# Block-sparse attention and a top-1 MoE on one core: wider exponential tiles, filler matmuls in four early steps, and one of the x copies moved to VectorE

## The chip, the cores and the metric

The kernel runs on one core of one Trainium2 chip. The metric is the device time of one execution in microseconds (us), as the median of several runs. Times inside an execution are in us from the start of its span, and durations of single instructions are in ns where that is said.

## The reference, cut to what matters

The inputs are q, k, v of shape (4, 8, 768, 64), that is 4 batches, 8 heads, 768 positions and a head size of 64, and the weights of an MoE with 8 experts. Everything is fp32.

```python
k_sum = k.reshape(B, H, nb, 32, D).max(axis=3)
v_sum = v.reshape(B, H, nb, 32, D).mean(axis=3)
scores_l = where(|i - j| < 16, scale * q @ k.T, -1e9)
scores_s = scale * q @ k_sum.T + log(32)
a = softmax(concat([scores_l, scores_s]))
x = a @ concat([v, v_sum])
e[s] = argmax(x @ w_gate) where the local gate is below 0.5, else e[s-1]
out[s] = p[e] * relu(x[s] @ w1[e]) @ w2[e]
```

Each position attends to the 31 positions around it and to 24 block summaries. Its row of x (512 wide, all heads) then goes through one expert, 512 to 1024 to 512.

## The kernel before

**Attention** is done for 16 pairs of heads (4 batches by 4 pairs), and for each pair in two groups of three query tiles of 128 positions, so there are 32 groups, G = 0 to 31. A query tile is taken as two halves of 64 positions; each half sees a window of 96 keys and the 24 summaries, W = 120 columns. TensorE (PE) does three things for a group:

- `s_mm` (lines 286 and 292): adds a mask by a matmul with an identity and then multiplies q by the window, into a score tile in PSUM. There are two score tiles, used in turn.
- `t_stage` (through the helper `halves`, line 536): transposes the exponentials. They lie in `pr`, a tile of 128 positions by 2 heads by 3 tiles by WE = W + 1 = 121 columns; the last column is a constant one, which multiplies the 1e-9 of the softmax's denominator. Every transpose takes the exponentials of 64 positions as the stationary operand (64 rows, 121 columns) and a 64x64 identity as the moving one. Rows 0 to 63 and rows 64 to 127 of the array work side by side, each into its own PSUM bank, so 12 transposes are 6 pairs. For one group of each pair of heads two more transposes follow, of `va`, the sums of v, which have the same width. ScalarE (ACT) copies the two banks to `pt`, one after the other (line 538).
- `a_mm` (line 326): multiplies `pt` by the window of v, `vw`.

The groups are software-pipelined by hand: in step G of the loop PE is given `s_mm(G)`, `t_stage(G-2)` and `a_mm(G-3)` in this order. VectorE (DVE) finds the row maximum (`s_max`, line 298), ACT takes six exponentials of 128x120 (`s_exp`, line 306), and DVE divides by the denominator (`a_norm`, lines 337 and 338). GpSimd (POOL) prepares what later pairs need, in this order for each pair of heads: four copies of the v summaries into `vw` (line 264, they need `pt`), three copies of key windows into `kb` (line 255), two additions that fold v (line 241), and the key summaries into `kb` (line 258, they need a reduction on DVE, line 231). SP issues the loads of q, k, v and `vw`; how far they run ahead is set by the buffers (two of `kb`, `kp` and `vt`, three of q and `vw`). Every engine takes its instructions in order.

**Between attention steps** the work of the previous batch's MoE is inserted. After every batch but the last, in three steps that follow one another (G = 10, 11, 12 after the first batch, and 8 and 16 later), `x_two` takes two tiles of x (128 positions by 512) and transposes them for the gate, also through `halves`: 16 transposes of 64 rows by 128 columns into the same two PSUM banks, copied by ACT to `hs` as two copies of 128x512, c = 0 and c = 1. `x_logits` (lines 565 to 576) multiplies `hs` by the gate's weights in these steps and the next two. The routing itself is a long chain of small DVE instructions with a few PE steps.

**The MoE** starts with the last attention steps and takes the time from 125 us to the end: pairs of blocks of 128 tokens, whose matmuls split fp32 into a high and a low part (lines 1176 to 1178 and 1206 to 1208).

At the start of the program 44 matmuls of a zero tile `wz` (128x128, bf16, line 214) run before the first data arrive.

Of the kernel before, what the change touches and what calls it, by code (L numbers as in the profile page):

```python
# [19 lines left out]
P = 128  # L20
# [2 lines left out]
NB = S // 32  # L23
WL = 96
W = WL + NB
WE = W + 1
NU = S // P
NG = 3
GP = NU // NG
# [14 lines left out]
DRAINS = 5  # L44
OOB = 4096
WARM = 44

WFETCH = (21, 21, 22, 22, 26, 30)
WSPLIT = (25, 29)
# [25 lines left out]
class Kernel:  # L75
# [91 lines left out]
    def attention(self, tick, rows, tail):  # L167
        nc, tc, ident = self.nc, self.tc, self.ident
        with ExitStack() as ctx:
# [13 lines left out]
            vts, kss, vss = {}, {}, {}  # L183
            vas = [cst.tile([P, WE], F32, name=f"va{i}") for i in range(3)]

            def load_k(n):
                b, p = pairs[n]
                nc.sync.dma_start(out=kp[n % 2][:, 16:16 + S], in_=self.kT[b, p])
# [14 lines left out]
            for t in vas:  # L203
                nc.gpsimd.memset(t, 0.0)
            prs = [cst.tile([P, 2, NG, WE], F32, name=f"pr{i}") for i in range(2)]
            for t in prs:
                nc.gpsimd.memset(t[:, :, :, W:WE], 1.0)
            for t in kp:
                nc.vector.memset(t[:, 0:16], 0.0)
                nc.vector.memset(t[:, 16 + S:], 0.0)  # L210

            wb = self.bank("t")
            for _ in range(WARM):
                nc.tensor.matmul(out=wb[:, 0:P], lhsT=self.wz, rhs=self.wz, start=True, stop=True)
            load_k(0)
            nc.scalar.dma_start(out=me, in_=self.maskc)

# [3 lines left out]
            t, src = next(consts)  # L221
# [49 lines left out]
            def s_mm(G):  # L271

                n, g = groups[G]
                sp = live[G] = self.score[G % 2].tile([P, 2, 512], F32, name="bs")
                quarters = [(h, c) for c in range(2) for h in range(2)]

                def at(h, c):
                    u = sp[64 * c:64 * c + 64, h, 0:NG * W].rearrange("p (u w) -> p u w", u=NG)  # L280
                    return slice(64 * h, 64 * h + 64), u

                for h, c in quarters:
                    r, o = at(h, c)
                    m0 = W * (2 * g + c)
                    nc.tensor.matmul(out=o.rearrange("p u w -> p (u w)"), lhsT=eye2[r], rhs=mask2[r, m0:m0 + NG * W],
                                     start=True, stop=False)
                for u in range(NG):
                    for h, c in quarters:
                        r, o = at(h, c)  # L290
                        t = 2 * (NG * g + u) + c
                        nc.tensor.matmul(out=o[:, u, :], lhsT=qs[n % 3][r, 64 * t:64 * t + 64], rhs=kb[n % 2][r, t, :],
                                         start=False, stop=(u == NG - 1))
# [16 lines left out]
            def t_stage(G, n=None):  # L310
                pr = live[G]
                pt = live[G] = wk.tile([WE, 2 * NG + 1, P], F32, name="pt", bufs=3)
                srcs = [pr[:, h, u, :] for h in range(2) for u in range(NG)]
                if n is not None:
                    srcs.append(vas[n % 3])
                    vss[n] = pt[0:NB, 2 * NG, :]
                self.halves(srcs, WE, pt[:, 0:len(srcs)])

            def a_mm(G):
# [3 lines left out]
                for u in range(NG):  # L323
                    for h in range(2):
                        for c in range(2):
                            nc.tensor.matmul(out=ap[64 * c:64 * c + 64, u, h, :], lhsT=pt[:, NG * h + u, 64 * c:64 * c + 64],
                                             rhs=vw[n % 3][0:WE, 2 * (NG * g + u) + c, h, :], start=True, stop=True)

# [25 lines left out]
            for G in range(last_g):  # L354
                if G == last_g - GP - 1:
                    ctx3.close()
                s_mm(G)
                tick(G, 2)
                tick(G, 4)
# [5 lines left out]
                if LT <= G:  # L365
                    n = G // 2 - 1 if G in (2, 4) else G // GP if G > 2 * GP and G % GP == 0 or G == 2 * GP + 1 else None
# [12 lines left out]
                n, g = divmod(G, GP)  # L379
# [145 lines left out]
            self.nc.tensor.transpose(out=m[:, P * c:P * c + P], in_=x[:, u % NG, P * c:P * c + P], identity=self.ident)  # L525
        return m

    def halves(self, srcs, m, dst):

        half = P // 2  # L530
        n = len(srcs)
        banks = [self.bank("t")[:m, 0:half * n].rearrange("p (i q) -> p i q", q=half) for c in range(2)]
        for i, src in enumerate(srcs):
            for c in range(2):
                r = slice(half * c, half * c + half)
                self.nc.tensor.transpose(out=banks[c][:, i], in_=src[r], identity=self.ident[r, r])  # L536
        for c in range(2):
            self.nc.scalar.copy(out=dst[:, :, half * c:half * c + half], in_=banks[c])  # L538

    def hs_of(self, b, u):  # L540
        if (b, u // 2) not in self.hs:
# [8 lines left out]
    def x_two(self, b, u):  # L550

        self.hs_of(b, u)
        srcs = [self.xs[b, v // NG][:, v % NG, P * c:P * c + P] for v in (u, u + 1) for c in range(KT)]
        self.halves(srcs, P, self.hs[b, u // 2].rearrange("p j k t -> p (j k) t"))

    def x_logits(self, b, g):

# [1074 lines left out]
```

## Time and profile before

| | |
|---|---|
| runs | 444.4, 445.69 and 446.58 us, median 445.69 |
| the profiled execution | 447.26 us |
| its span, first to last instruction | 445.5 us |
| mean granted clock of TensorE | 0.981 of 2.4 GHz |
| PE busy | 423.7 us (95%) |
| weight loads (PEld) busy | 371.2 us (83%) |
| DVE, ACT, POOL busy | 242.1, 201.0 and 214.8 us |
| moved by DMA | 95.87 MB, mean 215 GB/s |

The profile is of one execution, and its span leaves out 1.8 us that lie around it. A busy PE is not a PE at its peak: matmuls overlap in the array, and several small ones side by side count as one busy time. The clock has two levels, 2.4 GHz (a granted clock of 1.00) and 1.2 GHz (0.50); a value between the two means that part of the stretch ran at the lower one.

### The profile page before, as it was taken

How to read it: one execution, taken by the hardware profiler on the slowest of the kernel's cores; microseconds unless marked ns; L12 is line 12 of the kernel's file. 1: busy time of each engine (PE TensorE's matmuls, PEld its weight loads, DVE VectorE, ACT ScalarE, POOL GpSimd, SP SyncE). 2: the span in 40 equal slices, each digit the busy share in tenths (PEclk: the TensorE clock that was granted, in tenths of full speed). 3: DMA queues.
4: the chain of work that ended last, by engine and by line, in shares of the span. 5: the costliest groups of instructions: out<-in, count | busy, mean ns of one | idle time of the engine just before them, and what ended most of it. 6: DMA issues, size and time to landing. Idle time of an engine off the chain costs nothing. (4 is left out here: it accounts for less than half of the span.)

```text
span 445.5 us, 12679 instructions
## 1 busy us (share of the span) xinstructions
PE 423.7 (95%) x4750; PEld 371.2 (83%) x4750; DVE 242.1 (54%) x577; ACT 201.0 (45%) x441; POOL 214.8 (48%) x310
## 2 busy tenths in 40 slices
PE   7989999988999999999999999999999999999992
PEld 6867788777889889898989889889897898978982
DVE  4657578797668578976531221223736652164720
ACT  3848678686865322712121201114536731276610
POOL 3387567568721430872012210211939792077960
PEclk9669999999999999999999999999999999999998
DMA  8899989999516192156056047200573876029581
GB/s 299 338 366 321 391 288 313 359 385 407 169 49 237 49 381 93 61 214 270 25 214 267 31 141 310 72 29 16 206 253 118 358 276 246 24 59 380 213 325 57
DMA packets 24007, 95.87 MB, mean 215 GB/s; under 512 B 2894, under 2 KB 3536, under 8 KB 19312
## 3 DMA queue, kind: packets, MB, share of 16 engines
q1 hardware_dynamic: 19328, 80.30, 48.4%
q0 software_dynamic: 4448, 14.29, 9.3%
q8 instruction: 44, 0.72, 0.7%
q14 instruction: 43, 0.35, 0.2%
q10 hardware_dynamic: 144, 0.20, 0.1%
HBM read 82.20 MB, written 12.71 MB: 213 GB/s over the span
## 5 line engine op out<-in xcount | busy, mean ns | idle before, releaser
L1206 PE MATMUL bs<-xT,h 128*128 128x256 f32 x352 | 101.6, 289 | 0.0
L1207 PE MATMUL bs<-xT,h 128*128 128x256 f32 x352 | 99.7, 283 | 0.0
L1208 PE MATMUL bs<-xT,l 128*128 128x256 f32 x352 | 99.6, 283 | 0.0
L1145 POOL DMA_INDIRECT xg<-x_dram,gidx x30 | 33.5, 1117 | 85.6 <-PE bt L1156 30.2
L1139 POOL TENSOR_TENSOR l<-stg,h 128x256 fp32r<-128x256 f32 x72 | 66.8, 963 | 15.3 <-ACT h L1131 14.7
L1176 PE MATMUL ba<-h,hT 128*128 128x512 f32 x176 | 71.5, 406 | 0.4
L1212 ACT ACTIVATE hT<-bs 128x512 fp32r<-128x512 f32 x44 | 26.3, 597 | 96.5 <-PE bs L1208 93.3
L1178 PE MATMUL ba<-h,hT 128*128 128x512 f32 x176 | 68.9, 392 | 0.0
L1177 PE MATMUL ba<-l,hT 128*128 128x512 f32 x176 | 68.8, 391 | 0.0
L1206 PEld LDWEIGHTS bs<-xT,h 128*128 128x128 f32 x352 | 67.5, 192 | 1.5 <-issue 0.8
L1207 PEld LDWEIGHTS bs<-xT,h 128*128 128x128 f32 x352 | 67.5, 192 | 0.3
L1214 DVE SCALAR_TENSOR_TENSOR hT<-bs,hT 128x512 fp32r<-128x512 f32 x44 | 30.4, 691 | 68.3 <-ACT hT L1212 56.0
L1208 PEld LDWEIGHTS bs<-xT,l 128*128 128x128 f32 x352 | 67.5, 192 | 0.0
L306 ACT ACTIVATE pr<-bs,nm 128x120 f32<-128x120 f32 x192 | 52.3, 389 | 6.0 <-DVE nm L298 3.9
L1131 ACT CAST h<-stg 128x1024 fp32r<-128x1024 f32 x48 | 49.0, 1051 | 9.3 <-PE ba L1178 7.6
L1192 POOL DMA_INDIRECT out_dram<-yo,sidx x24 | 25.0, 1043 | 49.6 <-DMA out_dram<-yo,sidx 12.0
L1134 DVE TENSOR_TENSOR l<-stg,h 128x1024 fp32r<-128x1024 f32 x30 | 40.2, 1351 | 12.6 <-ACT h L1131 9.4
L538 ACT COPY pt<-bt 121x448 f32<-121x448 f32 (+1 forms) x64 | 29.4, 515 | 25.4 <-PE bt L536 23.4
L1176 PEld LDWEIGHTS ba<-h,hT 128*128 128x128 f32 x176 | 33.2, 188 | 7.4 <-issue 0.6
L1178 PEld LDWEIGHTS ba<-h,hT 128*128 128x128 f32 x176 | 33.1, 188 | 7.2
L1177 PEld LDWEIGHTS ba<-l,hT 128*128 128x128 f32 x176 | 33.2, 189 | 5.6
L264 POOL COPY vw<-pt 24x384 f32<-24x384 f32 x64 | 30.3, 514 | 8.9 <-ACT pt L538 8.0
(307 smaller groups left out, 673.8 us busy)
## 6 DMA issues: line engine op xcount, KB each, us to landing
stg<-in_w SPq DMA_DIRECT2D x28, 1024.0 KB, 7.3
vw<-in_vW SPq DMA_DIRECT2D x16, 780.0 KB, 6.7
few_w<-in_w SPq DMA_DIRECT2D x8, 1024.0 KB, 8.1
kp<-in_kT SPq DMA_DIRECT2D x16, 384.0 KB, 6.7
q<-in_qT SPq DMA_DIRECT2D x16, 384.0 KB, 7.3
vt<-in_vT SPq DMA_DIRECT2D x16, 384.0 KB, 7.2
x_dram<-xs SPq DMA_DIRECT2D x8, 768.0 KB, 5.4
wst<-in_w SPq DMA_DIRECT2D x8, 512.0 KB, 6.6
```

Of the source, the lines that this page charges most:

```text
L306: nc.scalar.activation(out=pr[:, h, u, 0:W], in_=sp[:, h, u, :], func=AF.Exp, bias=nm[:, h, u:u + 1], scale=1.0)
L1131: self.nc.scalar.copy(out=hi, in_=src)
L1134: eng.tensor_tensor(out=lo, in0=src, in1=hi.bitcast(F32), op=ALU.subtract)
L1139: eng.tensor_tensor(out=lo[:, p], in0=src[:, p], in1=hi[:, p].bitcast(F32), op=ALU.subtract)
L1145: self.nc.gpsimd.indirect_dma_start(out=t, out_offset=None, in_=rows, in_offset=bass.IndirectOffsetOnAxis(ap=self.gidx[:, i:i + 1], axis=0))
L1176: nc.tensor.matmul(out=ps, lhsT=ah, rhs=wh, start=first, stop=False)
L1177: nc.tensor.matmul(out=ps, lhsT=ah, rhs=wl, start=False, stop=False)
L1178: nc.tensor.matmul(out=ps, lhsT=al, rhs=wh, start=False, stop=last)
L1206: nc.tensor.matmul(out=ps[:, j], lhsT=wh, rhs=xh, start=(k == 0), stop=False)
L1207: nc.tensor.matmul(out=ps[:, j], lhsT=wh, rhs=xl, start=False, stop=False)
L1208: nc.tensor.matmul(out=ps[:, j], lhsT=wl, rhs=xh, start=False, stop=(k == KT - 1))
L1214: nc.vector.scalar_tensor_tensor(out=l, in0=ps, scalar=0.0, in1=h.bitcast(F32), op0=ALU.max, op1=ALU.subtract)
```

## The change

It has three parts.

1. WE becomes W + 4 = 124. The exponentials' tiles `pr` and the sums `va` are 124 columns wide, with zeros in the three new ones, and so is every transpose of them; `pt` has 124 rows and `a_mm` contracts over 124. The exponentials themselves still write 120 columns.
2. Before `s_mm(G)` for G = 2, 3, 6 and 7, PE multiplies the zero tile by itself 20, 8, 8 and 8 times, into the bank "m".
3. In `x_two`, DVE makes the copy c = 1 and ACT the copy c = 0.

```diff
-WE = W + 1
+WE = W + 4
+FILL = {2: 20, 3: 8, 6: 8, 7: 8}
...
-                nc.gpsimd.memset(t[:, :, :, W:WE], 1.0)
+                nc.gpsimd.memset(t[:, :, :, W:WE], 0.0)
+                nc.gpsimd.memset(t[:, :, :, W:W + 1], 1.0)
...
-            wb = self.bank("t")
-            for _ in range(WARM):
-                nc.tensor.matmul(out=wb[:, 0:P], lhsT=self.wz, rhs=self.wz, start=True, stop=True)
+            def warm(n, bank):
+                wb = self.bank(bank)
+                for _ in range(n):
+                    nc.tensor.matmul(out=wb[:, 0:P], lhsT=self.wz, rhs=self.wz, start=True, stop=True)
+
+            warm(WARM, "t")
...
+                if G in FILL:
+                    warm(FILL[G], "m")
                 s_mm(G)
...
-    def halves(self, srcs, m, dst):
+    def halves(self, srcs, m, dst, both=False):
...
         for c in range(2):
-            self.nc.scalar.copy(out=dst[:, :, half * c:half * c + half], in_=banks[c])
+            copy = self.nc.vector.tensor_copy if c and both else self.nc.scalar.copy
+            copy(out=dst[:, :, half * c:half * c + half], in_=banks[c])
...
-        self.halves(srcs, P, self.hs[b, u // 2].rearrange("p j k t -> p (j k) t"))
+        self.halves(srcs, P, self.hs[b, u // 2].rearrange("p j k t -> p (j k) t"), True)
```

In the orders below, line numbers of the changed kernel are those of its own text: 217 is the zero matmul, 291 and 297 are `s_mm`, 303 the maximum, 342 and 343 `a_norm`, 543 and 546 the transposes and copies of `halves`, 236 and 239 the reductions of k and v.

On PE, steps G = 2 and 3 before (bs is a score tile, me the mask, bt one of the two banks of transposes):

```order
L292 MATMUL bs<-kb_143,q_140 64x120 x12
...
L286 LDWEIGHTS me
L286 MATMUL bs<-me 64x360
...
L292 MATMUL bs<-kb_144,q_141 64x120 x12
L536 MATMUL bt<-ident,pr_160 121x64 x12
L536 MATMUL bt<-ident,va_154 121x64 x2
L286 LDWEIGHTS me
```

And now:

```order
L297 MATMUL bs<-kb_143,q_140 64x120 x12
L217 LDWEIGHTS wz
L217 MATMUL bm<-wz 128x128
...
L291 LDWEIGHTS me
L291 MATMUL bs<-me 64x360
...
L297 MATMUL bs<-kb_144,q_141 64x120 x12
L543 MATMUL bt<-ident,pr_160 124x64 x12
L543 MATMUL bt<-ident,va_154 124x64 x2
L217 LDWEIGHTS wz
L217 MATMUL bm<-wz 128x128
...
L291 LDWEIGHTS me
```

The zero matmuls (20 the first time, 8 the second) stand ahead of the mask matmuls of `s_mm`; nothing else has moved on PE. They stand in the same way ahead of `s_mm(6)` and `s_mm(7)`, each time behind the matmuls of `a_mm`.

On DVE, step G = 10 with the first `x_two`, before (nm is the row maximum, ks a reduction of k, xs is x):

```order
L337 RECIPROCAL dn<-ba 128x6
L338 TENSOR_TENSOR xs<-ba,dn 128x3x128
L231 TENSOR_REDUCE ks<-kp_148 128x24
L298 TENSOR_REDUCE nm<-bs 128x6
L234 TENSOR_REDUCE va_154<-vt 128x24
```

And now (hs is what `x_two` writes):

```order
L342 RECIPROCAL dn<-ba 128x6
L343 TENSOR_TENSOR xs<-ba,dn 128x3x128
L236 TENSOR_REDUCE ks<-kp_148 128x24
L546 COPY hs_956<-bt 128x8x64
L303 TENSOR_REDUCE nm<-bs 128x6
L239 TENSOR_REDUCE va_154<-vt 128x24
```

Each of the nine `x_two` leaves one copy on ACT, and the other now stands on DVE behind `a_norm` (and a reduction of k, in every second step) and ahead of the next maximum. On ACT one copy of 128x512 stands at that place where there were two.

## Rows read from the trace of the kernel before

**Rows 1.** Busy us by stretch: PE, PEld, DVE, ACT, POOL; clock, DMA share, GB/s
```profile
0.00:33.80 33.80, 27.81 (x468) 24.18 (x469) 19.04 (x33) 18.87 (x58) 17.33 (x49) 0.80 0.90 334
33.80:62.80 29.00, 27.15 (x623) 22.76 (x619) 18.17 (x38) 22.80 (x73) 18.44 (x39) 1.00 0.93 333
62.80:91.92 29.12, 27.66 (x629) 23.25 (x626) 24.81 (x64) 22.73 (x73) 20.00 (x41) 1.00 0.96 338
91.92:124.93 33.01, 29.95 (x650) 24.94 (x646) 26.66 (x71) 24.85 (x75) 26.45 (x48) 1.00 0.83 309
```

**Rows 2.** Waits of PE from 125 us to the end: total, times, longest
```profile
PE bm L565 <- ACT hs L548: 0.3, 1, 0.3
```

**Rows 3.** Waits of PE from 0 to 125 us
```profile
PE bs L286 <- ACT pr L306: 2.6, 2, 1.9
PE bt L536 <- ACT hs L538: 2.3, 10, 0.4
PE bm L565 <- ACT hs L538: 1.4, 3, 0.5
PE bs L292 <- POOL kb L258: 1.3, 2, 1.2
```

**Rows 4.** Line 536, weight loads and matmuls: ns min/median/max, first and last start
```profile
L536 PEld LDWEIGHTS bt<-ident,pr x384: 176/182/323, 10.8 to 130.1; 64*121 64x121 f32 x192
L536 PE MATMUL bt<-ident,pr x384: 213/266/460, 10.8 to 130.2; 64*121 64x64 f32 x192
L536 PEld LDWEIGHTS bt<-ident,xs x144: 134/138/142, 42.3 to 113.0; 64*128 64x128 f32 x144
L536 PE MATMUL bt<-ident,xs x144: 214/223/276, 42.3 to 113.1; 64*128 64x64 f32 x144
```

**Rows 5.** Other fp32 weight loads, grouped by line: busy us, mean ns | idle before
```profile
L1206 PEld LDWEIGHTS bs<-xT,h 128*128 128x128 f32 x352 | 67.5, 192 | 1.5 <-issue 0.8
...
L609 PEld LDWEIGHTS bm<-ident,val 128*6 128x6 f32 x4 | 0.3, 83 | 0.5 <-DVE val L606 0.3
```

**Rows 6.** Timeline of PE, two bursts of transposes that nothing held up: start, length
```profile
67.06 0.85 PE L536 MATMUL bt<-ident,pr 64*121 64x64 f32 x12
...
71.78 0.71 PE L536 MATMUL bt<-ident,xs 64*128 64x64 f32 x16
```

**Rows 7.** Stretches at the lower clock, and two plain steps; columns of rows 1
```profile
12.40:18.60 6.20, 6.13 (x92) 5.27 (x91) 3.56 (x6) 5.33 (x18) 2.75 (x6) 0.50 0.95 380
25.70:32.00 6.30, 6.25 (x92) 5.35 (x92) 3.33 (x7) 2.81 (x10) 4.41 (x9) 0.50 1.02 386
33.80:39.00 5.20, 5.20 (x136) 4.59 (x133) 4.09 (x8) 4.92 (x17) 3.89 (x9) 1.00 0.99 352
```

**Rows 8.** Timeline of PE where steps 2, 3, 6 and 7 begin
```profile
9.48 0.35 PE L286 MATMUL bs<-me 64*64 64x360 bf16 x4 [1.90 <-ACT pr L306]
...
12.46 0.51 PE L286 MATMUL bs<-me 64*64 64x360 bf16 x4 [0.73 <-ACT pr L306]
...
25.75 1.48 PE L292 MATMUL bs<-kb,q 64*64 64x120 f32 x24 [1.16 <-POOL kb L258]
...
30.27 0.51 PE L286 MATMUL bs<-me 64*64 64x360 bf16 x4
```

**Rows 9.** Timeline of POOL, first and last row of its work before step 6
```profile
20.80 1.85 POOL L264 COPY vw<-pt 24x384 f32<-24x384 f32 x4 [4.57 <-ACT pt L538]
...
25.27 0.43 POOL L258 TENSOR_SCALAR kb<-ks 128x288 f32<-128x288 f32 x1
```

**Rows 10.** The zero matmuls at the start, by line
```profile
L214 PE MATMUL bt<-wz 128*128 128x128 bf16 x44 | 4.6, 304 | 1.0 <-DVE kp L210 1.0
```

**Rows 11.** Timeline of ACT, the two copies of the first x_two
```profile
43.91 1.13 ACT L538 COPY hs<-bt 128x512 f32<-128x512 f32 x2
```

**Rows 12.** Timeline of PE, the wait of the transposes' second bank
```profile
45.09 0.84 PE L536 MATMUL bt<-ident,pr 64*121 64x64 f32 x11 [0.17 <-ACT hs L538]
```

**Rows 13.** The nearest DVE instruction that reads 128x512 in PSUM
```profile
L1214 DVE SCALAR_TENSOR_TENSOR hT<-bs,hT 128x512 fp32r<-128x512 f32 x44 | 30.4, 691 | 68.3 <-ACT hT L1212 56.0
```

## The prediction

> **What bounds the kernel now.** I read the busy time by stretch first, then the waits of PE, then the two kinds of transposes, and last the early steps in order of time.
>
> The span falls into two parts. From 125 us to the end PE hardly waits: four waits are listed there, the longest 0.3 us [rows 2]. Nothing of the change lies in that part, so it will begin earlier or later by what attention gains or loses, and keep its length. All of the answer lies in the first 125 us.
>
> There, too, PE is the busiest engine: 27.15 of 29.00, 27.66 of 29.12 and 29.95 of 33.01 us in the three stretches after 33.8 us [rows 1]. Its waits are few. It waits for the copies of x on ACT 2.3 us (10 times) in the transposes and 1.4 us (3 times) in the gate's matmuls, and in the early steps for the exponentials (2.6 us) and for POOL's key windows (1.3 us) [rows 3]. But the others are close: ACT is busy 4.92 of 5.20 us over two plain steps [rows 7], and the DMA engines 0.93 and 0.96 of the two stretches from 33.8 to 91.92 us [rows 1]. What PE saves can be used only as far as these allow. The first 33.8 us have a granted clock of 0.80 [rows 1]: two pieces of 6.2 and 6.3 us ran wholly at 1.2 GHz, with PE busy nearly all the time [rows 7].
>
> **Part 1: the width of 124.** The trace has both widths through the same line. A weight load of 121 columns takes 182 ns and its matmul 266; of 128 columns, 138 and 223 [rows 4]. The wider one is the shorter one. In time that counts, 12 transposes of 121 take 0.85 us and 16 of 128 take 0.71 us where nothing holds them up [rows 6]. Per pair that is (0.85 - 0.27) / 5 = 0.116 us against (0.71 - 0.22) / 7 = 0.070. A burst of 12 at the quick rate would take 5 x 0.070 + 0.22 = 0.57 us, 0.28 less, and half of the bursts have one more pair, 0.046 more. So PE saves 32 x 0.28 + 16 x 0.046 = **9.7 us** if 124 behaves as 128.
>
> No row shows 124. The other bound is that it behaves as 121, with three more columns: from 6 columns to 121 the load grows by (182 - 83) / 115 = 0.86 ns a column [rows 4, 5], so 2.6 ns a load and about 0.5 us lost over 208 pairs. A plain fp32 load of 128 columns takes 192 ns [rows 5], and the 121-wide transposes lie on that slow line, so the quick way is open to a transpose of some widths only. 121 is odd, 124 divides by 4 as 128 does; I take the quick value because 124 is nearest to 128 in both size and divisibility, and keep the other for the range and as a rival.
>
> The Trainium skill's page "TensorE: Matmul & The Clock Gate", section "LDWEIGHTS (loading the stationary operand)", speaks against this part: it gives the time of a load as columns divided by 1.2 GHz, so that three more columns would cost 2.5 ns each time and nothing could be saved. The trace disagrees with it where it can be asked: 128 columns take 44 ns less than 121 [rows 4].
>
> How much of 9.7 us reaches the end? Of 32 bursts, 6 lie in the first 33.8 us and are left to part 2. Fifteen lie in the steps with work on x (G = 10 to 14 and the same later), where PE has the most to do: 15 x 0.30 = 4.5 us. In the other 11, ACT is next: two plain steps can shrink from 5.20 to its 4.92 us [rows 7], so 0.14 a step: 1.5 us. Together **6.0 us**.
>
> **Part 2: the zero matmuls.** They fill gaps so that the clock stays up. Before, the gaps were 1.90 us ahead of step 2, 0.73 ahead of step 3 and 1.16 inside step 6; ahead of step 7 there is none [rows 8]. At the start of the program 44 of them took 4.6 us, 104 ns each, mostly at 1.2 GHz [rows 10]; half that at 2.4 GHz. So 20 cost 1.0 to 2.1 us and fit the first gap but for 0.2 us at most, 8 cost 0.4 to 0.8 and fit the second. In step 6 they stand ahead of the masks, and the wait for POOL behind them shrinks by as much. If that cover goes, because POOL comes earlier, they cost 0.4 to 0.8 us there. In step 7 they cost that for certain: **-0.5 us**.
>
> What they can bring: the two pieces at 1.2 GHz, 12.5 us, hold 6.2 us of excess. Not all can be had. Behind the first piece step 6 waits for POOL, which works through 20.80 to 25.70 us without a pause (five rows, the first and the last in [rows 9]) and starts it when ACT has copied `pt`, so only what brings that copy forward counts, which I put at half of 3.1 us. Of the second, 3.1 us, all counts. That gives at most 4.6 us; nothing, if the clock falls all the same. The granted clock fell after gaps, and those inside the steps (PE waiting for POOL or DVE) are not filled. I take **2.0 us**, a little less than the middle.
>
> **Part 3: the copies of x.** ACT's two copies take 1.13 us one after the other [rows 11]. With the second on DVE at the same time, the wait of the second bank, 0.17 us [rows 12], six times, falls away (1.0 us), and so do the three waits of the gate's matmuls, which need both copies (1.4 us) [rows 3]: **2.4 us**. The bounds are 0 and all 3.7 us. The copy itself costs DVE between 0.56 us (half of ACT's two) and 0.69 us [rows 11, 13]; I take 0.65, near the row of the same engine. Nine are 5.9 us, 2.0 in each stretch, where DVE has 10.8, 4.3 and 6.3 us idle [rows 1]; that idle time hides it. Queued behind it is the next maximum, and behind that the exponentials; if DVE were late, each copy would push them by 0.65 us.
>
> **What is late next.** From 33.8 to 91.92 us PE would save 10 x 0.30 + 6 x 0.14 + 1.6 = 5.4 us, but the DMA engines are idle for only 2.0 + 1.2 = 3.2 us there [rows 1]. I take off the difference, **-2.2 us**. In the last stretch (0.83) there is room.
>
> **The sum**: 6.0 + 2.4 + 2.0 - 0.5 - 2.2 = 7.7 us. The profiled execution took 447.26 us, so it would take 439.6. It lies 1.6 us above the median of the runs shown, 445.69; against that median the forecast is **438.0 us**.
>
> **The rivals.**
>
> *124 is as slow as 121.* For it: the only quick width in the trace is 128. Against it: 121 is the only slow width of a transpose with more than a few columns, and it is odd. Then part 1 gives -0.5 us, DMA limits nothing, and 2.4 + 2.0 - 0.5 - 0.5 = 3.4 us are left: 442.3 us.
>
> *The loads set the pace all through attention.* For it: DMA at 0.90 to 0.96 until 91.92 us, behind loads that wait for buffers. Against it: PE's list shows no wait for a load, and POOL, which needs the data first, reaches PE in 1.3 us only [rows 3]. The deciding point is when POOL's waits for k and v grow longer than its lead over `s_mm`. Then the gain is the 3.2 us of idle DMA: 442.5 us.
>
> *DVE sets the pace* (the other side). Its busy time is 24.81 of 29.12 us in the third stretch of four where a routing chain runs [rows 1]. If the steps already move as fast as DVE does, then PE's savings in parts 1 and 3 come to nothing, and nine copies add 9 x 0.65 = 5.9 us; 1.5 us of part 2 remain: 447.3 + 4.4 = 451.7 us, against the median 450.1. It decides where DVE's idle time ahead of the copy is under 0.65 us. Against it: PE lists no long wait for DVE, and in the stretch before, DVE is idle for 10.8 us.
>
> That the zero matmuls do not hold the clock is within the forecast: 7.7 - 2.0 = 5.7 us, 440.0.
>
> **How the numbers follow.** Forecast 0.64, with a range of its own of 434 to 441 (clock held wholly and no limit by DMA at the low end, clock lost and a tighter ACT at the high end); slow 124, 0.20; loads, 0.11; DVE, 0.05. A measurement tells about 0.5%, 2.2 us, from no change. Faster by more than that: all of the forecast, three quarters of slow 124 and six tenths of the loads, 0.64 + 0.15 + 0.06 = 0.85. Within: 0.10. Slower: 0.05. The range reaches from 433.8 to 443.8 us, over the middle two rivals, and leaves out the third and the far ends.
>
> **What would show it.** Right: weight loads of the exponentials at about 138 ns instead of 182, bursts of 12 at about 0.6 us; a granted clock above 0.9 in the first stretch and step 8 starting about 2 us before 33.8; no wait of the gate's matmuls for ACT; the part after attention as long as it was. Wrong: loads at 185 ns; the clock at 0.50 in the same places; PE waiting for POOL's key windows, behind POOL's waits for loads; maxima late behind DVE's copies.

## The result, and the profile after

The changed kernel took 441.85 us as the median of five runs (441.42 to 443.19), the kernel before 446.28 beside it (444.4 to 446.8): a ratio of 0.991, 95% interval 0.9883 to 0.9938, so 4.4 us less by the medians and 4.0 by the ratio. In a second comparison, later, the ratio was 0.9957 (0.9927 to 0.9988), about 2 us less. The forecast was 7.7 us less: the direction held and the time lies in the range (433.8 to 443.8), but the size did not hold.

The profiled execution took 443.19 us, the longest of the five, its span 441.3, against 447.26 and 445.5. The first matmul of the MoE's main part starts at 120.64 us instead of 124.93, and from there on PE again hardly waits:

```profile
PE bm L617 <- DVE val L614: 0.4, 1, 0.4
```

This is the longest of the five waits of PE listed from 120 us to the end; the others are 0.3 us or less, as in [rows 2]. All of the difference lies in attention, as the prediction said. Where in attention it lies is another matter. The next fence is the view of [rows 1] for the changed kernel, cut at the same places of the program: where steps 8, 16 and 24 begin, and where the MoE does.

```profile
0.00:28.32 28.32, 23.81 (x512) 20.54 (x512) 18.61 (x33) 18.64 (x58) 16.41 (x49) 1.00 0.95 357
28.32:58.65 30.33, 26.17 (x622) 21.64 (x619) 20.27 (x42) 21.25 (x70) 19.58 (x41) 0.94 0.97 359
58.65:88.09 29.44, 26.11 (x627) 21.51 (x625) 27.19 (x70) 21.46 (x71) 21.68 (x44) 1.00 0.97 351
88.09:120.64 32.55, 28.41 (x647) 23.35 (x645) 27.01 (x69) 23.20 (x71) 24.80 (x45) 0.95 0.80 290
```

The lengths were 33.80, 29.00, 29.12 and 33.01 us. The first stretch is 5.5 us shorter, at a granted clock of 1.00. The second is 1.3 us longer and the third 0.3 us longer, though PE is busy 1.0 and 1.6 us less in them; the fourth is 0.5 us shorter. So the gain is made early and about a quarter of it is given back. The DMA share of the first three stretches rose from 0.90, 0.93 and 0.96 to 0.95, 0.97 and 0.97.

The transposes became as quick as they were forecast to be. By line (the answer to [rows 4]):

```profile
L543 PEld LDWEIGHTS bt<-ident,pr x384: 132/137/225, 10.6 to 125.6; 64*124 64x124 f32 x192
L543 PE MATMUL bt<-ident,pr x384: 218/221/363, 10.6 to 125.7; 64*124 64x64 f32 x192
L543 PEld LDWEIGHTS bt<-ident,xs x144: 133/138/222, 37.0 to 109.1; 64*128 64x128 f32 x144
```

A load of 124 columns takes 137 ns where 121 took 182, as much as one of 128. The Trainium skill's page "TensorE: Matmul & The Clock Gate", section "LDWEIGHTS (loading the stationary operand)", makes a load longer with every column (columns by 1.2 GHz); the runs disagree, and the measurement decides.

The waits of PE from 0 to 125 us (the answer to [rows 3]; here and below the rows on the copies of x, and those that end at nothing that the profile shows, called "issue"):

```profile
PE ba L331 <- issue: 1.6, 1, 1.6
PE bm L573 <- DVE esel L799: 1.5, 1, 1.5
PE bs L297 <- issue: 1.4, 1, 1.4
PE bs L291 <- issue: 1.3, 1, 1.3
PE bm L573 <- issue: 1.2, 1, 1.2
PE bt L543 <- ACT hs L546: 1.0, 4, 0.4
PE bt L543 <- DVE hs L546: 0.6, 1, 0.6
PE bm L582 <- DVE g L858: 0.5, 1, 0.5
```

Two things are to be seen. The waits that come with the copies of x are 1.5 + 1.0 + 0.6 + 0.5 = 3.6 us; they were 3.7 [rows 3]. And "issue" is now 1.6 + 1.4 + 1.3 + 1.2 = 5.5 us, where the kernel before had three such waits, 1.7 us:

```profile
PE bs L292 <- issue: 1.1, 1, 1.1
PE bs L286 <- issue: 0.4, 1, 0.4
PE bt L536 <- issue: 0.2, 1, 0.2
```

The four of the changed kernel, here in the timeline of PE (start, length, then the idle time ahead of it):

```profile
33.00 0.43 PE L297 MATMUL bs<-kb,q 64*64 64x120 f32 x5 [1.42 <-issue]
...
39.64 0.31 PE L291 MATMUL bs<-me 64*64 64x360 bf16 x1 [1.35 <-issue]
...
47.02 0.41 PE L573 MATMUL bm<-hs,wg 128*32 128x128 f32 x2 [1.17 <-issue]
...
87.48 0.68 PE L331 MATMUL ba<-vw,pt 124*64 124x65 f32 x15 [1.61 <-issue]
```

PE stops in the middle of a group of like matmuls: 19 of 24 are done before the first gap, and then nothing is issued for 1.42 us. No tile is missing. What ends shortly before each gap's end is a packet of 16 KB on the DMA queue that carries instructions (44 of them in a whole execution, 19 in the first 125 us, about 1.03 us each):

```
kernel    PE idle, us        the packet before it ended, us    from there to PE's next matmul
changed   31.58 to 33.00     31.62                             1.38
changed   38.29 to 39.64     38.13                             1.51
changed   45.85 to 47.02     45.70                             1.32
changed   85.87 to 87.48     86.17                             1.31
before    39.28 to 39.70     38.42                             1.28
before    99.42 to 100.53    99.09                             1.44
```

So the reading is that PE has run out of instructions and waits for the next piece of its program, which travels on the same 16 DMA engines as the loads. The places of the gaps bear it out. Count what the trace has of PE's own instructions (weight loads, matmuls and its sequencer's) from 0, in order of time. The first behind each of the four gaps is number 1217, 1473, 1730 and 3521, and behind the two of the kernel before 1217 and 3778: each time a multiple of 256 further on, to within one. Call these places borders, and the 256 instructions between two of them a piece. In the seventeen profiles of this case (the two kernels and the fifteen runs below) PE has 78 such gaps of more than 0.35 us in the first 126 us. 71 of them stand at a border, whatever line of the kernel is there, and the same 71 end 1.2 to 1.6 us after a packet of that queue. A packet, then, brings a piece of 256 instructions, and PE stops at the border when its packet comes late. Whether it is late because the engines are full was the theory to test.

Two of the four gaps, those that end at 39.64 and 87.48, are followed by a fall of the clock; the other two are not:

```profile
40.50:43.90 3.40, 3.40 (x57) 3.05 (x59) 2.12 (x4) 2.38 (x8) 2.36 (x6) 0.51 1.03 387
88.40:91.70 3.30, 3.30 (x59) 2.66 (x53) 1.88 (x3) 2.05 (x7) 2.41 (x5) 0.50 1.02 406
```

PE is busy all through these 3.4 and 3.3 us, at 1.2 GHz, which is 1.7 us too long each.

### The profile page after: what moved, and what is told of

It reads as the page before. It is cut to its first block, busy times and chain, and to the rows that moved or that the text cites. A ratio compares the mean times of both kernels' runs of the same rounds, so it can differ in the third digit from the quotient of the medians.

```text
span 441.3 us, 12774 instructions
## 1 busy us (share of the span) xinstructions
PE 415.2 (94%) x4794; PEld 362.8 (82%) x4794; DVE 247.1 (56%) x586; ACT 196.3 (44%) x432; POOL 214.1 (49%) x312
## 5 line engine op out<-in xcount | busy, mean ns | idle before, releaser
L1147 POOL TENSOR_TENSOR l<-stg,h 128x256 fp32r<-128x256 f32 x72 | 64.9, 936 | 14.0 <-ACT h L1139 13.7
L1200 POOL DMA_INDIRECT out_dram<-yo,sidx x24 | 26.2, 1091 | 50.0 <-DMA out_dram<-yo,sidx 14.4
L546 ACT COPY pt<-bt 124x448 f32<-124x448 f32 (+1 forms) x64 | 29.9, 532 | 21.1 <-PE bt L543 20.0
```

The source lines that it names most:

```text
L1147: eng.tensor_tensor(out=lo[:, p], in0=src[:, p], in1=hi[:, p].bitcast(F32), op=ALU.subtract)
```

## The experiments

Fifteen kernels were run, in four groups; the kernels of a group ran on one chip with the kernel before beside them (medians 447.98, 445.65, 447.46 and 445.71 us). The ratio to it is given with its 95% interval, and "us less" is that ratio times the median beside it. The changed kernel's own ratio came out 0.5% apart in its two comparisons, so only kernels of one group, or of groups 1 and 3, which ran on the same chip, are compared closely. The part after attention took 320.6 us in the profile of the kernel before and 321.8 to 323.2 in the eight of groups 1 and 3, so profiles are compared only up to the start of the MoE (124.93 us before).

### Group 1: one part at a time, and lighter loads of v

The width alone:

```diff
-WE = W + 1
+WE = W + 4
...
-                nc.gpsimd.memset(t[:, :, :, W:WE], 1.0)
+                nc.gpsimd.memset(t[:, :, :, W:WE], 0.0)
+                nc.gpsimd.memset(t[:, :, :, W:W + 1], 1.0)
```

> The kernel before with part 1 alone (124 columns). Prediction's step: 6.0 us less, or 4 with the limit by DMA, with the two stretches at 1.2 GHz left in place. Theory of code fetch (PE runs out of instructions while all DMA engines are full, and the gap ends about 1.4 us after the packet of queue 8): 2 to 5 us less, and more than the 1.5 us of unexplained ('issue') gaps over 0.35 us that the kernel before shows up to 130 us. Theory that ACT or DVE sets the pace: 1 to 3 us less, issue gaps as before, and PE waiting for ACT or DVE in their place.

Measured: 442.61 us, ratio 0.9887 (0.9849 to 0.9926), 5.1 us less. But the two low stretches of the clock did not stay in place, as the expectation had them. The first 29.60 us, to step 8, in the view of [rows 1]:

```profile
0.00:29.60 29.60, 22.56 (x468) 19.47 (x468) 18.00 (x32) 18.75 (x58) 16.38 (x48) 0.94 0.91 348
```

Step 8 began 4.2 us earlier, with one piece of 3.4 us at 1.2 GHz (from 23.8 us on) in place of the two. The MoE began at 118.75 us, 6.2 us earlier, so only 2.0 us were won behind step 8. There PE was busy 78.9 us instead of 84.8; two thirds of those 5.8 us went into new waits. PE's waits for the exponentials in steps 2 and 3 were still there (2.9 us, the longest 1.9), and the clock did not fall behind them; why is not shown.

The zero matmuls alone:

```diff
+FILL = {2: 20, 3: 8, 6: 8, 7: 8}
...
+                if G in FILL:
+                    warm(FILL[G], "m")
                 s_mm(G)
```

> The kernel before with the zero matmuls alone. Prediction's step: 2.0 - 0.5 = 1.5 us less. From the profile of the changed kernel: step 8 begins 4 to 5 us earlier (33.8 before), the granted clock stays at 1.00 until step 8. Code fetch: part of that is lost again in issue gaps and in clock falls behind them, so 1 to 4 us less at the end. If nothing is lost later, 4 to 5 us less.

Measured: 445.55 us, ratio 0.9958 (0.9932 to 0.9984), 1.9 us less. The clock held until the MoE; the first 29.19 us, to step 8, in the view of [rows 1]:

```profile
0.00:29.19 29.19, 24.77 (x512) 21.24 (x512) 18.78 (x33) 18.80 (x58) 16.31 (x47) 1.00 0.94 351
```

Step 8 began 4.6 us earlier and the MoE also 4.6 us earlier, at 120.32 us: behind step 8 nothing was won and nothing lost.

The second copy of x on DVE alone:

```diff
-            self.nc.scalar.copy(out=dst[:, :, half * c:half * c + half], in_=banks[c])
+            copy = self.nc.vector.tensor_copy if c and both else self.nc.scalar.copy
+            copy(out=dst[:, :, half * c:half * c + half], in_=banks[c])
```

> The kernel before with one of two copies of x on VectorE alone. Prediction's step: 2.4 us less; PE's waits for ACT's copies of x (3.7 us) fall to about 1.3. Code fetch: 0 to 2 us less, since what PE saves in the steps with x comes where the DMA engines are full. DVE as the pace: slower by up to 5.9 us.

Measured: 449.96 us, ratio 1.0055 (1.0019 to 1.0092), 2.5 us more, where the prediction had 2.4 less. PE's waits on the copies of x, 0 to 125 us:

```profile
PE bm L566 <- DVE hs L539: 1.4, 1, 1.4
PE bt L536 <- ACT hs L539: 1.3, 4, 0.4
...
PE bt L536 <- DVE hs L539: 0.7, 1, 0.7
PE bm L575 <- DVE g L851: 0.5, 1, 0.5
```

They come to 3.9 us, no fewer than the 3.7 of before. Part of the loss shows in the clock: the mean of this profiled execution (452.89 us, one of the longer ones) is 0.966, and beside the two low pieces of before there are others, these two (the view of [rows 7]):

```profile
58.60:62.00 3.40, 3.40 (x58) 2.80 (x56) 2.23 (x7) 2.49 (x8) 0.00 (x0) 0.50 0.30 70
96.20:102.90 6.70, 6.70 (x96) 5.72 (x94) 4.58 (x12) 4.47 (x14) 2.60 (x7) 0.50 0.94 373
```

Over its twelve executions the median of the mean clock is 0.977, and 0.980 in the kernel before beside it; that difference is worth about 1.3 us (an estimate: 0.003 of the time). What makes the clock fall there was not tried, and the rest of the 2.5 us stays open.

The fourth kernel was to make the loads lighter: the changed kernel with only the 96 partitions of `vw` loaded that change, from the fourth pair on (the rest of the tile stays from the first three loads or is written by POOL; the result is the same).

```diff
-                nc.sync.dma_start(out=vw[n % 3], in_=self.vW[b, p])
+                r = P if n < 3 else WL
+                nc.sync.dma_start(out=vw[n % 3][0:r], in_=self.vW[b, p, 0:r])
```

> The changed kernel, but from the fourth pair of heads on only 96 of 128 partitions of vw are loaded: the other rows are constant and stay in the buffers (nothing is left out of the result). 13 loads of 780 KB become 585 KB, 2.5 MB of 41 MB. Code fetch: the issue gaps of 7.1 us fall by a third or more, and the time by 2 to 4 us against the changed kernel. Loads as the pace through late data: also 2 to 4 us less, but issue gaps as they are. ACT or DVE as the pace: no change (within 1 us of the changed kernel).

Measured: 455.08 us, ratio 1.0175 (1.0124 to 1.0227): 7.8 us more than the kernel before, a clear miss. The edit removed bytes and yet filled the DMA engines. The stretch from 28 to 120 us of the changed kernel, and then of this one (last columns: clock, DMA share, GB/s):

```profile
28.00:120.00 92.00, 80.51 (x1891) 66.32 (x1887) 74.19 (x178) 66.22 (x211) 65.71 (x128) 0.96 0.91 333
```

```profile
28.00:120.00 92.00, 76.20 (x1748) 63.04 (x1747) 69.58 (x164) 60.57 (x193) 58.96 (x117) 0.93 1.00 302
```

The share is 1.00 while fewer bytes a second arrive. A packet of 6240 bytes of `vw` took 409 ns here (median of the 1114 that start from 28 to 120 us), 238 in the changed kernel (of 1536). And the waits that end at "issue" doubled:

```profile
PE ba L332 <- issue: 5.7, 4, 2.0
PE bs L298 <- issue: 3.1, 3, 2.1
PE bs L292 <- issue: 2.3, 2, 1.9
...
PE bt L544 <- issue: 0.6, 1, 0.6
```

That is 11.7 us, 6.2 more than the 5.5 of the changed kernel. Meant as the opposite, the run speaks for the theory: fuller DMA engines, longer gaps. It does not say why the packets became slower.

### Group 2: two parts at a time, and fewer loads of q

Width and zero matmuls, with the copies left on ACT (the first two diffs of group 1 together):

> The kernel before with the width of 124 and the zero matmuls, and both copies of x left on ACT. If the three parts add up (alone they measured about -5.1, -1.9 and +2.5 us against 447.98), this takes 6 to 7 us off the kernel before, about 0.985 of it, and is some 2 to 2.5 us quicker than the changed kernel. Rival: the parts share one limit, the loads; then removing the third part gives nothing and it stays within 1 us of the changed kernel (0.991).

Measured: 442.24 us, ratio 0.9921 (0.9893 to 0.9949), 3.5 us less. The parts do not add up to 7. The rival is right that something is shared, but what the profiles show to be shared is the time ahead of step 8. That step begins at 29.49 us here (29.24 in the repeat of group 3), where the width alone reached it at 29.60 and the zero matmuls alone at 29.19, from 33.80 before. Each part alone wins the same 4 us or so ahead of step 8, and they can be won once. Behind step 8 this kernel wins 1.5 us (0.7 in the repeat), the width alone 2.0, the zero matmuls alone nothing.

Width and copy, without the zero matmuls (the first and third diffs):

> The kernel before with the width of 124 and the second copy of x on DVE, without the zero matmuls. If the parts add up: -5.1 + 2.5, about 2.6 us less than the kernel before (0.994). Rival: the copy on DVE costs only while PE is slow at 121 columns (it then shifts clock falls); then with 124 it costs nothing or gains up to 1 us, and this stands at 0.987 or below, no worse than the width alone (0.9887).

Measured: 443.43 us, ratio 0.9936 (0.9905 to 0.9968), 2.9 us less. This is the sum of the two parts alone.

Then the loads themselves. The changed kernel with q loaded only for the first three pairs:

```diff
-                nc.sync.dma_start(out=qs[n % 3], in_=self.qT[b, p])
+                if n < 3:
+                    nc.sync.dma_start(out=qs[n % 3], in_=self.qT[b, p])
```

> The changed kernel with q loaded for the first three pairs only (13 loads of 384 KB left out, so the scores of later pairs use the q of earlier ones): all of the same work on the engines, 5.1 MB of about 41 MB less on the DMA engines in attention. Theory (full DMA engines delay the fetch of PE's instructions, and the gaps that PE then shows without a wait, 7.1 us in the changed kernel, ate the gain): these gaps fall under 2 us in all and the time falls by 4 to 6 us below the changed kernel, to about 0.98 of the kernel before. Rival (ACT and DVE set the pace of the steps and the gaps would have been waits anyway): the gaps go, but waits for ACT or DVE take their place, and the time falls by under 1.5 us.

Measured: 437.79 us, ratio 0.983 (0.9792 to 0.9868), 7.6 us less than before and some 3.5 us less than the changed kernel's 0.991. (The 7.1 us of gaps in the expectation held 1.5 us that the list of waits puts down to a copy on DVE; by that list it is 5.5.) DMA engines and waits of PE:

```profile
28.00:120.00 92.00, 83.42 (x1991) 69.06 (x1991) 78.73 (x200) 69.68 (x223) 66.69 (x130) 1.00 0.80 289
```

```profile
PE bs L298 <- issue: 0.8, 1, 0.8
```

With a share of 0.80 instead of 0.91, "issue" falls from 5.5 to 0.8 us, the clock stays at 1.00 over these 92 us, and DVE and ACT do 4.5 and 3.5 us more work in the same time (which reaches 5 us into the MoE there): they did not set the pace. The MoE begins at 114.80 instead of 120.64 us, and with its 321.0 us it is no shorter, so the gain lies in attention. The same edit on the kernel before:

> The kernel before with the same 13 loads of q left out. PE shows only 1.5 us of gaps without a wait there, so by the theory of delayed instruction fetch it gains 1 to 2 us (0.996). Rival (loads set the pace of attention in both kernels): it gains as much as the changed kernel does by the same edit.

Measured: 446.75 us, ratio 1.0011 (0.9991 to 1.0032): nothing. Its "issue" waits fell only from 1.7 to 1.2 us (0.9 and 0.3). So the loads cost the kernel before nothing that can be measured, and the changed one several us.

### Group 3: copies of x and loads, two by two on one chip

> The changed kernel again, on the chip of the three runs beside it, so that they can be compared without a change of chip: 0.991 of the kernel before, as in its first comparison.

Measured: 445.45 us, ratio 0.9957 (0.9927 to 0.9988). Width and zero matmuls without the copy on DVE:

> Width and zero matmuls without the copy on DVE, beside the changed kernel on one chip. If the copy on DVE gains as the prediction says, this is 2.4 us slower than the changed kernel. Theory (the copies on ACT overlap, so that little waiting is won, and late copies on DVE make new waits): within 1 us of it. Rival (the copy costs what it cost alone, 2.5 us): 2 us or more quicker.

Measured: 444.17 us, ratio 0.9939 (0.9914 to 0.9963). The same without the 13 loads of q:

```diff
-                nc.sync.dma_start(out=qs[n % 3], in_=self.qT[b, p])
+                if n < 3:
+                    nc.sync.dma_start(out=qs[n % 3], in_=self.qT[b, p])
```

> Width and zero matmuls without the copy on DVE and without the 13 loads of q, as in the changed kernel without them. Beside it this gives the price of the copy on DVE where the loads set no pace: 2.4 us slower than the changed kernel without the loads by the prediction, within 1 us by the theory of late copies, quicker if DVE's time is what counts then.

Measured: 440.24 us, ratio 0.985 (0.9829 to 0.9871). And the changed kernel without these loads:

> The changed kernel without the 13 loads of q again, on the same chip as the changed kernel: 3 to 4.5 us quicker than that if the loads take what the gaps in PE's instructions show, 0.982 of the kernel before; no more than 2.2 us quicker by the size that the prediction gave the loads.

Measured: 440.76 us, ratio 0.9863 (0.9836 to 0.9889). The gaps shrank but did not all go: "issue" is 3.1 us in this profile and 2.3 in the one without the copy, where the same two kernels with all loads have 6.2 and 7.2.

| median, us | copy on DVE | copies on ACT | copy on DVE costs |
|---|---|---|---|
| with all loads | 445.45 | 444.17 | 1.3 |
| without the 13 loads of q | 440.76 | 440.24 | 0.5 |
| the loads cost | 4.7 | 3.9 | |

The ratios give the loads a price of 0.0094 and 0.0089, 4.2 and 4.0 us, with an uncertainty of about 1.8 and 1.5 us from the intervals. That is about twice the 2.2 us of the prediction. The copy on DVE costs 0.8 and 0.6 us by the ratios, within their uncertainty nothing; by the same intervals it brings no more than about 1 us in either row, so the 2.4 us of the prediction are excluded.

### Group 4: the late copies, and the place of the weight loads

Left open were why the copies on DVE bring nothing, and whether it is the fullness of the DMA engines at a time that counts. First the changed kernel with two of the nine second copies back on ACT:

```diff
-        self.halves(srcs, P, self.hs[b, u // 2].rearrange("p j k t -> p (j k) t"), True)
+        self.halves(srcs, P, self.hs[b, u // 2].rearrange("p j k t -> p (j k) t"), (b, u) not in ((1, 0), (2, 2)))
```

> The changed kernel with the second copy back on ACT in two of the nine x_two, the first of the second batch and the second of the third, where VectorE came 0.8 and 1.5 us after ACT. Theory (late copies make the new waits): PE's waits for VectorE's copy (0.6 us) and for the argmax of the gate (1.5 us) go, and the time falls by 0 to 2 us below the changed kernel (0.991), less where the loads take it. Rival (VectorE's time costs in every step): the waits move to other places and the time stays.

Measured: 441.14 us, ratio 0.9884 (0.9844 to 0.9923). The waits that come with the copies of x:

```profile
PE bm L573 <- ACT hs L546: 0.7, 1, 0.7
PE bm L582 <- DVE g L858: 0.7, 1, 0.7
PE bt L543 <- ACT hs L546: 0.2, 1, 0.2
```

1.6 us instead of 3.6: the two late copies made the new waits. Whether the time fell is not resolved, as the interval takes in the changed kernel's 0.991; "issue" in this execution is 2.7 + 2.2 + 2.2 + 0.8 + 0.5 = 8.4 us, more than the waits that were won.

Second, width and zero matmuls with copies on ACT, and the loads of expert weights spread:

```diff
-WFETCH = (21, 21, 22, 22, 26, 30)
+WFETCH = (22, 25, 26, 27, 28, 30)
```

> Width and zero matmuls, copies on ACT, and the first four loads of expert weights (512 KB each), which went out in steps 21 and 22, spread over steps 22, 25, 26 and 27, the fifth from 26 to 28. No byte less is loaded. Theory (full DMA engines hold up PE's instructions): the gap of about 1.4 us that all runs with both widths and fillers show near 86 us goes, the DMA share between 80 and 90 us falls, and the time falls by 0.5 to 1.5 us below that without the move (0.992). Rival (a fixed place where PE's instructions run out): the gap stays.

Measured: 442.79 us, ratio 0.9919 (0.9885 to 0.9953), no different from 0.9921 without the move. The DMA share from 80 to 90 us did fall, here without the edit (group 2) and then with it:

```profile
80.00:90.00 10.00, 8.59 (x222) 7.20 (x222) 8.85 (x24) 7.37 (x25) 8.45 (x17) 1.00 1.01 387
```

```profile
80.00:90.00 10.00, 8.85 (x223) 7.23 (x222) 8.40 (x23) 6.64 (x23) 7.10 (x14) 1.00 0.79 290
```

No gap of over 0.5 us stands near 86 us in this profile, but one of 0.73 us does at 82, and the sum of "issue" is 1.3 + 1.2 + 1.1 + 0.9 + 0.6 = 5.1 us against 5.6. The expectation was mistaken about the gap, though: neither profile of the kernel without this edit (groups 2 and 3) has one between 77 and 94 us, though the first has a DMA share of 1.01 from 80 to 90 us. So this run does not decide. Both edits on the changed kernel:

> Both edits together on the changed kernel: seven copies on VectorE, weight loads spread. If the waits won add up, 1 to 3 us below the changed kernel, 0.985 to 0.989 of the kernel before, and below both kernels.

Measured: 441.62 us, ratio 0.9889 (0.9843 to 0.9934), the same as with the first edit alone. The expected band of 0.985 to 0.989 is met at its end, but neither of the new versions is shown to be faster than the changed kernel: the lowest ratio, 0.9884, lies in the interval of the changed kernel's first comparison (0.9883 to 0.9938). The width alone (0.9887, 0.9849 to 0.9926) does so too, but against the repeat of the changed kernel on the same chip (0.9957, 0.9927 to 0.9988) it is the quicker one by 0.0070, with an uncertainty of 0.0050 from the intervals: 3 us. Beside the width the other two parts brought nothing there, and rather cost time.

## Why the prediction was right or wrong

**The time lies in the range by luck.** The sum of the prediction puts 2.0 - 0.5 = 1.5 us ahead of step 8 and 6.0 + 2.4 - 2.2 = 6.2 us behind it. The profile of the changed kernel has 5.5 us won ahead of step 8 and 1.2 us lost behind it. The first is 4.0 us more than forecast, the second 7.4 us less, and what was left of the two stayed within the range. Up to the MoE the profiles (one execution each; a second figure is the repeat's) read, in us:

| kernel | start to step 8 | step 8 to the MoE |
|---|---|---|
| before | 33.80 | 91.13 |
| width alone | 29.60 | 89.15 |
| zero matmuls alone | 29.19 | 91.13 |
| copy on DVE alone (a long execution) | 32.83 | 95.79 |
| width and zero matmuls | 29.49, 29.24 | 89.60, 90.47 |
| width and copy | 29.30 | 89.59 |
| changed: all three | 28.32, 28.94 | 92.32, 91.84 |
| changed, without 13 loads of q | 29.25, 28.32 | 85.55, 88.02 |
| width and zero matmuls, without them | 28.30 | 87.01 |
| before, without them | 33.98 | 89.96 |

**Right: that the part after attention keeps its length.** It took 320.6 us before and 320.7 now.

**Width: right in the burst, wrong in where it counts.** 124 behaves as 128, and the rival "124 is as slow as 121" is out. A burst of 12 that nothing holds up takes 0.58 us instead of 0.85 [rows 6]; 0.57 was forecast:

```profile
26.97 0.58 PE L543 MATMUL bt<-ident,pr 64*124 64x64 f32 x12
```

Alone it brings 5.1 us (3.3 to 6.8), and the term was 6.0, but this is a coincidence. The term counts the bursts behind 33.8 us alone, and there the width won 2.0 us; 4.2 us came from the first stretch, where the prediction gave it nothing ("left to part 2"). The step that failed is the one from what PE saves to what reaches the end. PE did save 5.8 us behind step 8; 3.9 of them became waits.

**Zero matmuls: right alone, nothing to be seen on top of the width.** The net term was 2.0 - 0.5 = 1.5 us, and alone they brought 1.9 (0.7 to 3.0). The sum adds them to the width, and that failed: the time that the low clock had cost ahead of step 8 is won by the width nearly as well, 4.2 us against 4.6, and both together win 4.3 to 5.5. The eight in step 7 cost what was said, 0.4 to 0.8 us. In the timeline of the changed kernel they delay the masks of that step by 0.55 us:

```profile
25.53 0.62 PE L217 MATMUL bm<-wz 128*128 128x128 bf16 x8
26.08 0.35 PE L291 MATMUL bs<-me 64*64 64x360 bf16 x4
```

They also have a price that the sum does not have. They put 88 instructions (44 matmuls and their weight loads) into PE's program ahead of step 8, so that the border at number 1217 comes 88 instructions sooner in the kernel's own work. In all twelve profiles of kernels with the zero matmuls PE stands still at that border, at 32.8 to 34.2 us, for 0.80 to 2.14 us, with the loads of q or without them; in the five without zero matmuls it does so for 0.51 us at most. Nor did they hold the clock every time: in three of the twelve it fell to 1.2 GHz for 3.4 us from about 22 us on. PE's wait for the key windows in step 6 was 0.91 us behind the fillers, where 1.16 stood before [rows 8], though the masks of that step came 2.2 us earlier (22.08 instead of 24.24), so POOL came forward too.

**Wrong: part 3, "2.4 us".** Alone the copy cost 2.5 us; in the changed kernel it is worth nothing that can be measured, and rather a loss. Two steps failed. The first: "ACT's two copies take 1.13 us one after the other". They overlap: in the trace of before each of them lasts 0.64 to 0.66 us and the second starts 0.47 after the first. On DVE the copy takes 0.68 us (0.65 was taken) and starts 0.03 to 0.11 us behind ACT's in five of the nine places, so that it ends about 0.35 us sooner there than ACT's second copy would. The second: "that idle time hides it". The idle time of a stretch says nothing about the moment. In two of nine places DVE came 0.83 and 1.49 us after ACT. This is DVE's timeline at the second of them; ACT had begun its copy at 103.70:

```profile
103.17 0.94 DVE L691 TENSOR_TENSOR A<-c,lanf 128x768 bf16<-128x768 f32 x1
104.04 0.54 DVE L239 TENSOR_REDUCE va<-vt 128x24 f32<-128x384 f32 x1
104.50 0.18 DVE L342 RECIPROCAL dn<-ba 128x6 f32<-128x6 f32 x1
104.71 0.56 DVE L343 TENSOR_TENSOR xs<-ba,dn 128x384 f32<-128x384 f32 x1
105.19 0.68 DVE L546 COPY hs<-bt 128x512 f32<-128x512 f32 x1
```

And PE, in the gate's matmuls (the releaser named, `esel`, is the next instruction on DVE; the copy ended at 105.87):

```profile
106.02 1.03 PE L573 MATMUL bm<-hs,wg 128*32 128x128 f32 x20 [1.54 <-DVE esel L799]
```

The copy stands behind a step of the routing, a reduction of v and the division, in an order that the section on the change shows for step 10, where no routing runs. This is the mechanism of the rival "DVE sets the pace", in two places instead of in every step; where those two copies went back to ACT, their waits went.

**Wrong in size and in kind: what the loads take, "-2.2 us".** Leaving out 13 loads of q, about an eighth of the bytes, brings back 4.0 to 4.2 us on one chip, each with an uncertainty of nearly half; what all loads together take was not measured. The step that failed took the loads as a limit on the sum of what PE saves: 3.2 us, the time in which the DMA engines were idle from 33.8 to 91.92 us. None of the kernels with all the loads reached that limit. From step 8 to step 24 the changed kernel lost 1.7 us (59.77 instead of 58.12), while with the same loads the width alone won 1.5 us there and width and copy 2.5. The rival "the loads set the pace all through attention" caps the whole gain at those 3.2 us. Its 442.5 us lie close to the result, but it is not right: with all the loads the width alone reached the MoE 6.2 us earlier, and its runs took 5.1 us less (3.3 to 6.8). Nor was POOL's lateness, its deciding point, what cost the time: PE's longest wait for POOL behind step 8 is 0.3 us. The loads take their time another way: PE's next packet of instructions comes late.

This can be read from the kept profiles. Between two borders exactly one packet of that queue starts, in each of the 204 pieces looked at (twelve in each profile, from instruction 961 to 4033). The time from PE's first instruction behind a border to the start of that packet is 1.8 us in the 27 pieces where the DMA share of the 3 us after the border is under 0.8, 2.5 us in the 67 from 0.8 to 1.0, and 3.6 us in the 110 above. By kernel (means over the twelve pieces):

| kernel | DMA share | border to packet, us | "issue", us |
|---|---|---|---|
| before | 0.96 | 2.6 | 1.7 |
| changed | 0.98, 0.96 | 3.4, 3.4 | 5.5, 6.2 |
| width and zero matmuls | 0.98, 0.97 | 3.5, 3.5 | 5.6, 7.2 |
| changed, without 13 loads of q | 0.90, 0.92 | 2.3, 2.6 | 0.8, 3.1 |
| width and zero matmuls, without them | 0.91 | 2.5 | 2.3 |
| changed, 96 partitions of `vw` | 0.99 | 4.0 | 11.7 |

The mean share does not settle it alone (0.96 stands there with 2.6 and with 3.4). A packet then takes 1.0 us, and PE goes on about 1.4 us after its end. In the changed kernel that makes 3.4 + 1.0 + 1.4 = 5.8 us, more than the 5.6 us that PE needs for a piece when it does not stop; without the loads of q it is 4.7 to 5.1 against about 5.5, in the kernel before 2.6 + 1.1 + 1.4 = 5.1 against 6.0. So the loads and the quicker PE make the gaps together, and the kernel before, slower in its pieces, lost nothing to them.

How sure is that? Shown: the gaps stand at the borders and nowhere else but for 7 of 78; with fewer loads the packets start sooner, the gaps shrink and some 4 us come back, in the changed kernel and in the one with both copies on ACT; the kernel before gains nothing by it. Not shown: the moment at which a packet is asked for (the border is taken for it), why the clock falls behind some gaps and not behind others, and what the rest of PE's savings behind step 8 went into. Moving 2 MB of weight loads lightened one place without changing the time.

**The failed steps together.** Behind step 8, of the 6.0 us for the width 2.0 came. Of the 2.4 for the copies nothing came: 89.59 us stand against 89.15 beside the width, and 1.4 to 2.7 us were lost beside the width and the zero matmuls. And the gaps in PE's instructions, for which the sum has no term, grew from 1.7 to 5.5 us. Ahead of step 8, 4.0 us more came than the sum has. The width, which the sum counts there as nothing, brings 4.2 us alone and the zero matmuls 4.6, and they do not add.

## What to carry to other kernels

Transposing 124 columns instead of 121 is a saving, so the number of columns of a stationary fp32 operand is worth a look (no other widths were tried). Two changes that win back the same lost time do not add: try each alone before both go into a sum, and say for each stretch what it is to bring. When PE gets faster in a stretch whose DMA engines are busy over 90%, look for the loss as "issue" gaps in the middle of a group of matmuls, not only as waits for tiles, and count whether they stand a multiple of 256 instructions apart, as they did here. Before a copy is moved to another engine, read that engine's queue at each place where the copy will stand, and check whether the two copies did not overlap already.

## What was not expected of the hardware

Loads of 96 partitions instead of 128 made the packets of 6240 bytes slower, 409 ns instead of 238, so that a quarter fewer bytes in these loads kept the DMA engines busier (share 1.00 instead of 0.91 from 28 to 120 us) and cost some 12 us against the changed kernel. And PE can stand still for 1.2 to 1.6 us in mid-group with every operand in place (up to 2.2 us in other runs), at every 256th of its instructions when the packet that brings the next ones is late, and goes on 1.2 to 1.6 us after that 16 KB packet has ended.
